# A linear-attention, FFN and soft-MoE kernel: the scheduler keeps TensorE's form, and the last block's weights use five, then six buffers

## The chip, the core and the metric

One NeuronCore of a Trainium2 chip runs the whole kernel. It has five engines that work in parallel, each through its own instruction queue in order: TensorE (PE, matmuls), VectorE (DVE), ScalarE (ACT), GpSimd (POOL) and SyncE (SP, which here only issues DMAs; ACT issues some too). The 16 DMA engines carry all queues' transfers. The metric is the device time of the kernel in microseconds (us); less is better.

## What is computed

The input goes through three stages. First, linear attention with positive features for 4 x 8 heads of 576 tokens, 64 wide, 128 features:

```python
h = proj - sq                       # proj = x @ omega.T, sq = |x|^2 / 2, x scaled by 64 ** -0.25
phi = np.exp(h - np.max(h, axis=-1, keepdims=True)) / np.sqrt(m)
kv = np.einsum('bhsm,bhsd->bhmd', k_p, v)
...
num / den                           # q_p @ kv over q_p @ sum(k_p), plus 1e-06
```

The result, 2304 tokens of 512 values, goes through a gated FFN with 1536 hidden values, and that through a soft mixture of 8 experts with 4 slots each:

```python
gate = 1.0 / (1.0 + np.exp(-(x @ w_gate)))
x = gate * (x @ w_val) @ w_out
logits = x @ phi
d = softmax(logits, axis=0)         # over tokens: what goes into each slot
slot_input = d.T @ x
slot_out[e] = np.maximum(slot_input[e] @ w1[e], 0.0) @ w2[e]
c = softmax(logits, axis=1)         # over slots
out = c @ slot_out
```

## The kernel before

**Tiling.** The FFN runs over five blocks of tokens: four of 512 (blocks 0 to 3) and a last one, block 4, of 256. Each block has 12 steps `f`, one for 128 of the hidden values. In a step, `gate` (PSUM tile `ga`), `val` (`va`) and `down` (`o0` to `o3`) each make 12 products: four chunks times the three of `three`, which multiplies numbers split into a high and a low part of type fp32r (hi by hi, hi by lo, lo by hi). So a step is three groups of twelve products, 512 columns wide, 256 in block 4; a step's `down` is done after the next step's `gate` and `val`. The soft-MoE's work on a finished block (`chunk_logits`, `chunk_x2`, `chunk_ltT`, `chunk_slot`) is done while the next block's FFN runs, in plain fp32, as are attention's products and all transposes. In the trace a plain fp32 product leaves two records, an fp32r product or a transpose one.

**Weights.** The weights of a step are three parts: gate (part 0), value (1), down (2). For the last blocks they come from the DRAM scratch `wscr` into `WR` (name `ws`), six slots of 256 KB. `split_w` makes the high part on ACT (or DVE) and the low one on POOL (or DVE) into tiles `w`, which the products read. In block 4 (`i >= LAST`) the parts come one by one in the order of the list `USE`: f0's gate and value, f1's, f0's down, f2's gate and value, f1's down, f3's gate (number 8) and value (9), f2's down, and so on. Only four slots serve them: number m goes into slot `m % 4`, and `split_w` of a part issues the load of the part four numbers later:

```python
def load_part(m):
    if m < len(USE):
        W[USE[m]] = WR[:, m % 4, :]
        SP.dma_start(out=W[USE[m]], in_=wscr[USE[m][0] % NF][:, USE[m][1], :])
```

The other two slots (4 and 5) are given by `free_early` to the experts' second weights W2, twelve microseconds of planned time into block 4, along with one buffer `gt`.

**The block's transposition.** `chunk_x2` transposes block 3's result with four DVE instructions, writes each quarter to DRAM (`xscr`) and reads it back (`x2T<-xscr`). Both go on SP's queue, between the weight loads; `chunk_slot`'s four products, 512 columns wide, need what is read back.

**What sets the order.** Every instruction is recorded by `Plan` and put in order by `schedule()` before the kernel is built. It is a list scheduler that simulates the five engines with the prices of `cost()`. Each instruction has a key (its stream's planned time less a lead), and `pick` takes the ready one of the lowest key on the engine that is free. `cost()` charges TURN = 0.2 extra for a bundle (`together`) of PE work with fewer than 128 rows, and 0.12 for products with 64 output partitions; no price hangs on what was issued before. A DMA is planned to land at 340 GB/s plus 2.0 us. All instructions are issued by one line of `issue`, so every row of the trace reads L413 (L449 in the changed kernel), and tile names tell the steps apart. W1, the experts' first weights, is loaded by `load_w1` on ACT's queue in pieces of 512 KB (`XT<-in_w` among them), W2 by `load_w2` on SP's. `join_slots` joins the blocks' running softmax before the tail.

## Time and profile before

| | |
|---|---|
| median of 3 runs (677.37, 679.89, 680.16) | 679.89 us |
| the profiled execution, its own time | 678.63 us |
| its span, first to last instruction | 676.8 us |
| PE busy | 658.8 us, 97% |
| DVE, ACT, POOL busy | 442.5, 429.0, 279.9 us |
| DMA moved | 147.90 MB, mean 219 GB/s |
| mean granted TensorE clock | 0.995 of full speed |

The share of busy time is an average over stages: attention and FFN run together in the first 200 us, then the FFN with the soft-MoE's chunks; block 4 lies at about 557 to 624 us; behind it is the experts' tail. The timeline lists groups of instructions of one kind with their start, their length from first start to last end, a count of records, and in brackets the idle time of the engine before the group with what ended it. Groups on PE overlap by some tenths at their ends, since matmuls are pipelined and their ends are modelled; the distance from one start to the next is what a group costs.

### The profile page before, as it was taken

How to read it: one execution, taken by the hardware profiler on the slowest of the kernel's cores; microseconds unless marked ns; L12 is line 12 of the kernel's file. 1: busy time of each engine (PE TensorE's matmuls, PEld its weight loads, DVE VectorE, ACT ScalarE, POOL GpSimd, SP SyncE). 2: the span in 40 equal slices, each digit the busy share in tenths (PEclk: the TensorE clock that was granted, in tenths of full speed). 3: DMA queues.
4: the chain of work that ended last, by engine and by line, in shares of the span. 5: the costliest groups of instructions: out<-in, count | busy, mean ns of one | idle time of the engine just before them, and what ended most of it. 6: DMA issues, size and time to landing. Idle time of an engine off the chain costs nothing.

```text
span 676.8 us, 12606 instructions
## 1 busy us (share of the span) xinstructions
PE 658.8 (97%) x4340; PEld 529.8 (78%) x4340; DVE 442.5 (65%) x1309; ACT 429.0 (63%) x965; POOL 279.9 (41%) x244
## 2 busy tenths in 40 slices
PE   7999999999999999999999999999999999999995
PEld 6676777878888888887888888788888788798663
DVE  3899999899997476666576555567343336575323
ACT  5899898888886765667566766455444445575012
POOL 1465445465444443444345343444444444443100
PEclk9999999999999999999999999999999999899998
DMA  8889876787975345834395222789833339966978
GB/s 285 314 269 341 277 252 226 250 273 242 309 252 171 123 153 193 243 126 162 101 260 167 89 67 75 255 295 334 251 93 101 101 107 310 284 207 233 406 303 240
DMA packets 57103, 147.90 MB, mean 219 GB/s; under 512 B 6096, under 2 KB 14032, under 8 KB 57040
## 3 DMA queue, kind: packets, MB, share of 16 engines
q1 hardware_dynamic: 51232, 129.74, 58.2%
q10 hardware_dynamic: 5808, 17.37, 7.7%
q8 instruction: 34, 0.56, 0.3%
q14 instruction: 29, 0.24, 0.1%
HBM read 128.73 MB, written 18.35 MB: 217 GB/s over the span
## 4 chain that ended last, share of the span: by engine, by line
PE 88%; DMA 4%; DVE 3%; ACT 2%; issue 1%; SPq 1%; POOL 0%; DVEq 0%; ACTq 0%; POOLq 0%
PE o L413 26%; PE ga L413 23%; PE va L413 23%; PE fl L413 16%; DMA g<-in_tok 1%; ACT g L413 1%; DMA ws<-wscr 1%; DVE g L413 1%; DMA g<-in_wall 1%; DMA xscr<-x 1%; DVE x2T L413 1%; SPq L413 1%; POOL g L413 0%; DVE g1b L413 0%; DVE ga_a L413 0%
## 5 line engine op out<-in xcount | busy, mean ns | idle before, releaser
L413 POOL TENSOR_TENSOR w<-ws,w 128x512 fp32r<-128x512 f32 x133 | 174.7, 1315 | 243.4 <-ACT w L413 115.6
L413 PE MATMUL ga<-XT,w 128*128 128x512 f32 (+1 forms) x720 | 169.8, 378 | 1.8 <-ACT w L413 0.8
L413 PE MATMUL va<-XT,w 128*128 128x512 f32 (+1 forms) x720 | 168.6, 376 | 1.8 <-ACT w L413 1.8
L413 PE MATMUL o<-gt,w 128*128 128x512 f32 (+1 forms) x720 | 167.4, 376 | 0.8 <-DVE gt L413 0.8
L413 PEld LDWEIGHTS o<-gt,w 128*128 128x128 f32 x720 | 124.3, 189 | 28.8 <-issue 3.7
L413 PEld LDWEIGHTS ga<-XT,w 128*128 128x128 f32 x720 | 124.4, 190 | 27.2 <-issue 1.9
L413 PEld LDWEIGHTS va<-XT,w 128*128 128x128 f32 x720 | 125.0, 190 | 26.5 <-issue 2.4
L413 ACT ACTIVATE w<-ws 128x512 fp32r<-128x512 f32 x113 | 71.0, 628 | 62.3 <-PE o L413 22.5
L413 PE MATMUL fl<-g,g 64*128 64x128 f32 (+4 forms) x686 | 83.9, 314 | 2.2 <-DVE g L413 0.8
L413 ACT ACTIVATE ga_a<-ga_a 128x512 f32<-128x512 f32 (+1 forms) x120 | 69.9, 583 | 19.3 <-DVE ga_a L413 18.1
L413 PEld LDWEIGHTS fl<-g,g 64*128 64x128 f32 (+2 forms) x686 | 61.5, 183 | 22.7 <-issue 6.1
L413 ACT ACTIVATE g<-g 128x128 f32<-128x128 f32 (+3 forms) x203 | 72.3, 408 | 10.9 <-DVE g L413 6.3
L413 ACT ACTIVATE ga_a<-ga 128x512 f32<-128x512 f32 (+1 forms) x60 | 33.3, 554 | 68.0 <-PE ga L413 67.9
L413 DVE SCALAR_TENSOR_TENSOR ga_a<-ga,ga_a 128x512 f32<-128x512 f32 (+1 forms) x60 | 38.0, 634 | 42.0 <-ACT ga_a L413 41.9
L413 DVE CAST w<-ws 128x512 fp32r<-128x512 f32 x49 | 20.9, 426 | 54.9 <-PE ga L413 37.5
L413 DVE TENSOR_TENSOR ga_a<-va,ga_a 128x512 f32<-128x512 f32 (+1 forms) x60 | 38.0, 633 | 20.5 <-ACT ga_a L413 17.6
L413 ACT ACTIVATE x2T<-g 128x512 f32<-128x512 f32 x72 | 45.4, 665 | 4.0 <-DVE x L413 4.0
L413 ACT ACTIVATE g1b<-g1b,g 128x128 f32<-128x128 f32 x128 | 40.5, 389 | 5.0 <-DVE g L413 4.9
L413 ACT ACTIVATE ga_a<-ga_a,one_b 128x512 f32<-128x512 f32 (+1 forms) x60 | 40.7, 678 | 1.3
L413 DVE TENSOR_SCALAR x2T<-x2T 128x512 f32<-128x512 f32 (+1 forms) x72 | 38.6, 549 | 2.8 <-ACT x2T L413 2.7
L413 DVE TENSOR_TENSOR g<-fl,g 64x288 f32<-64x288 f32 (+3 forms) x61 | 29.3, 482 | 15.0 <-ACT g L413 13.9
L413 POOL TENSOR_TENSOR g<-g 128x640 f32<-128x640 f32 (+1 forms) x22 | 25.9, 1176 | 31.1 <-DVE g L413 17.5
(197 smaller groups left out, 789.5 us busy)
## 6 DMA issues: line engine op xcount, KB each, us to landing
ws<-wscr SPq DMA_DIRECT2D x42, 512.0 KB, 3.7
ws<-wscr SPq DMA_DIRECT2D x78, 256.0 KB, 3.1
g<-in_wall SPq DMA_DIRECT2D x36, 512.0 KB, 4.9
g<-in_von SPq DMA_DIRECT2D x16, 640.0 KB, 5.8
wscr<-x SPq DMA_DIRECT2D x36, 256.0 KB, 4.8
g<-in_qkT SPq DMA_DIRECT2D x15, 576.0 KB, 5.1
g<-in_tok SPq DMA_DIRECT2D x15, 576.0 KB, 5.3
g<-in_w ACTq DMA_DIRECT2D x16, 512.0 KB, 6.2
```

The source lines that it names most:

```text
L413: ins = getattr(self.eng[e], method)(*a, **k)
```

## The change

The change has two halves.

In the scheduler, `form()` gives each PE instruction its form: operand rows, output partitions, and whether it is fp32r. The new `pick_pe` takes the lowest key as before; but if that one's form differs from the form of the last instruction put on PE, it takes, among the ready ones of the last form, the lowest whose key is no more than STAY = 2.0 later, if there is one. In the simulated time a change of rows or output partitions costs SWITCH = 0.18 and a change to fp32r ROUND = 0.09; TURN and the 0.12 are gone from `cost()`'s PE prices. The planned landing of a write to `xscr` gets BACK = 1.5 more.

In the weights of block 4, the parts are taken from a list `todo` in the order of `USE`, and each goes into whichever slot has come free. Five loads are issued where four were (slots 0 to 4), a sixth (slot 5) after the split of the step before. Slots 4 and 5 stay in use until a part with number 15 (`WIDE`) or later has been split out of them; then `free_early` gives both to W2. `free_early` no longer hands out the `gt` buffer.

```diff
 LATE8 = 0.3
 FLOOR = 8
-EARLY = 12.0
+WIDE = 15
 SQP = [0, 0, 1, 1, 1, 0, 1, 0]
...
 SIZE = {F32: 4, F32R: 4, I32: 4, U32: 4, I64: 8}
 HOP = 0.16
+SWITCH = 0.18
+STAY = 2.0
+ROUND = 0.09
+BACK = 1.5
 TURN = 0.2
 ROWS = 4
...
         if method == "together":
-            return TURN * (eng == "PE" and kw["parts"][0][2][0].ap[0][1] < 128) + sum(self.cost(eng, a[1], a[3], o, i)[0] for a, o, i in kw["parts"]), False
+            return sum(self.cost(eng, a[1], a[3], o, i)[0] for a, o, i in kw["parts"]), False
         o = outs[0] if outs else None
         n = self.free(o) if o is not None else 0
...
                 return max(0.43 * n / 256, 0.055) / 4, False
             if o.ap[0][1] == 64:
-                return max(n / 600.0, 0.21) / 2 + 0.12, False
+                return max(n / 600.0, 0.21) / 2, False
             return max(0.222, n / 600.0) * (ins[0].ap[0][1] / 128 if o.ap[0][1] == 128 else 1.0), False
         ni = max([n] + [self.free(a) for a in ins])
...
         return 0.06, False
+    def form(self, i):
+        alts, _, _, _, outs, ins, _ = self.ops[i]
+        if alts[0][0] != "PE":
+            return None
+        kw = alts[0][3]
+        if "parts" in kw:
+            _, outs, ins = kw["parts"][0]
+        return ins[0].ap[0][1], outs[0].ap[0][1], ins[0].dtype == F32R
     def schedule(self):
...
             return self.cost(e, alt[1], alt[3], outs, ins)
+        forms = [self.form(i) for i in range(n)]
+        form = [(128, 128, False)]
+        def pick_pe():
+            while ready["PE"] and taken[ready["PE"][0][1]]:
+                heapq.heappop(ready["PE"])
+            if not ready["PE"]:
+                return None
+            x = ready["PE"][0]
+            if forms[x[1]] != form[0]:
+                same = [y for y in ready["PE"] if y[0] <= x[0] + STAY and forms[y[1]] == form[0] and not taken[y[1]]]
+                x = min(same, default=x)
+            ready["PE"].remove(x)
+            heapq.heapify(ready["PE"])
+            return x[1]
         def pick(e):
+            if e == "PE":
+                return pick_pe()
             shared = e in ("DVE", "POOL") and port > now + 1e-9
...
                     alt = next(a for a in alts if a[0] == e)
                     c, held = self.cost(e, alt[1], alt[3], outs, ins)
+                    if e == "PE" and forms[i] != form[0]:
+                        c += SWITCH * (forms[i][:2] != form[0][:2]) + ROUND * (forms[i][2] > form[0][2])
+                        form[0] = forms[i]
                     if held:
                         port = now + c
...
                         nb *= SIZE[outs[0].dtype]
                         dma = max(dma, now) + nb / 340e3
-                        end = max(dma, now + nb / 340e3) + 2.0
+                        end = max(dma, now + nb / 340e3) + 2.0 + BACK * outs[0].tensor.name.startswith("xscr")
                     order.append((now, i, alt))
                     free_at[e] = now + c
...
     WR = T([128, 6, 512], "ws")
     W, Q, WS, G = {}, {}, {}, {}
+    spent = []
     cw = {}
...
     USE = [(i + (p < 2), p) for i in range(LAST - 1, NB * NF) for p in range(3) if LAST <= i + (p < 2) < NB * NF]
-    def load_part(m):
-        if m < len(USE):
-            W[USE[m]] = WR[:, m % 4, :]
+    slot, todo = {}, list(range(len(USE)))
+    def load_part(k):
+        if todo:
+            m = todo.pop(0)
+            slot[USE[m]] = k
+            W[USE[m]] = WR[:, k, :]
             SP.dma_start(out=W[USE[m]], in_=wscr[USE[m][0] % NF][:, USE[m][1], :])
...
                 W[i, p] = a[:, p, :]
         elif i == LAST:
-            for m in range(4):
-                load_part(m)
+            for k in range(5):
+                load_part(k)
     def load_q(n):
...
         lo_of(t[:, 1, :], w, t[:, 0, :], ("DVE",) if end else SITE["lw"])
         WS[i, part] = t
+        if (i, part) == (LAST - 1, 2):
+            load_part(5)
         if i >= LAST:
-            load_part(USE.index((i, part)) + 4)
+            k = slot[i, part]
+            if k < 4 or USE.index((i, part)) < WIDE:
+                load_part(k)
+            else:
+                spent.append(k)
+                if len(spent) == 2:
+                    free_early()
     def up_passes(i, part, tag):
...
     def free_early():
+        lead, plan.lead = plan.lead, LEAD["ex"]
         free.append(WR[:, 4:6, :].rearrange("p a c -> p (a c)"))
-        free.extend(pieces("gt", 2, 1))
         load_w2()
+        plan.lead = lead
     def free_halves():
...
             jobs += [(start + 10.0 + 12 * k, "ex", load_w1) for k in range(6)]
         if j == NB - 1:
-            jobs += [(start + 10.0, "ex", load_w1), (start + 40.0, "ex", free_more), (start + EARLY, "end", free_early),
+            jobs += [(start + 10.0, "ex", load_w1), (start + 40.0, "ex", free_more),
                      (start + span * 0.9, "end", free_halves), (start + span * 0.85, "m2", join_slots)]
         start += span
     jobs += moe_jobs(NB * NF, start, 1.0)
```

What moves, as the order of instructions on three engines tells it. SP, block 4, around the writes of block 3's transposed result (`xscr`) and the reads of it (`x2T<-xscr`), before; `ws<-wscr` are weight parts, `gt`, `x` and `more` W2 pieces:

```order
L413 DMA gt<-in_w 128x1024
L413 DMA xscr_75<-x_726 128x512
L413 DMA xscr_76<-x_726 128x512
L413 DMA xscr_77<-x_726 128x512
L413 DMA xscr_78<-x_726 128x512
L413 DMA ws<-wscr 128x512
L413 DMA x2T<-xscr_75 32x4x512
L413 DMA ws<-wscr 128x512
L413 DMA x2T<-xscr_76 32x4x512
```

The same place in the changed kernel:

```order
L449 DMA ws<-wscr 128x512 x8
L449 DMA gt<-in_w 128x1024
L449 DMA xscr_75<-x_726 128x512
L449 DMA xscr_76<-x_726 128x512
L449 DMA xscr_77<-x_726 128x512
L449 DMA xscr_78<-x_726 128x512
L449 DMA ws<-wscr 128x512 x2
L449 DMA x2T<-xscr_75 32x4x512
L449 DMA ws<-wscr 128x512
L449 DMA x2T<-xscr_76 32x4x512
```

Counted over block 4, eight weight parts stood ahead of the first write and now ten, nine ahead of the first read and now twelve.

PE, block 4, steps f3 to f5 (`w_733` is f4's gate part), with `chunk_slot`'s products `fl<-x2T,dt`, before:

```order
L413 MATMUL ga<-XT_105,w_733 128x256 x2
L413 MATMUL fl<-ident,cs 128x128
L413 MATMUL ga<-XT_105,w_733 128x256 x10
L413 MATMUL fl<-x2T,dt 32x512 x3
L413 MATMUL va<-XT_105,w_736 128x256 x2
L413 MATMUL fl<-x2T,dt 32x512
L413 MATMUL o_718<-gt,w_741 128x256 x2
```

The place of the same products in the changed kernel, six steps later (`w_768` is f9's gate part):

```order
L449 MATMUL ga<-XT_105,w_768 128x256 x12
L449 MATMUL va<-XT_105,w_771 128x256 x12
L449 MATMUL fl<-x2T,dt 32x512 x4
L449 MATMUL o_718<-gt,w_772 128x256 x3
L449 MATMUL o_719<-gt,w_772 128x256 x3
```

The four products stand in a row and later. In the same way block 3's sixteen logits' products, fifteen and one before, stand in a row, and the PE work of `join_slots` has moved from the middle of block 4 to its last step. Over the whole program PE changes rows or output partitions 127 times instead of 136 (five of the nine within the first 78 us, four in block 4), and type alone 121 times instead of 154.

ACT, the start of block 4 (`w_704` is f1's gate part, `x2T<-o` takes block 3's result out of PSUM), before:

```order
L413 DMA XT<-in_w 128x1024
L413 ACTIVATE ga_a<-ga 128x256
L413 ACTIVATE w_704<-ws 128x512
L413 ACTIVATE ga_a<-ga_a 128x256
L413 ACTIVATE ga_a<-ga_a,one_b 128x256
L413 ACTIVATE x2T<-o_614 128x512
```

The same place in the changed kernel:

```order
L449 DMA XT<-in_w 128x1024
L449 ACTIVATE ga_a<-ga 128x256
L449 ACTIVATE w_704<-ws 128x512
L449 ACTIVATE ga_a<-ga_a 128x256
L449 DMA XT<-in_w 128x1024
L449 ACTIVATE ga_a<-ga_a,one_b 128x256
```

A third piece of W1 is issued there that came behind the cast of `w_733` before; a fourth has moved to the cast of `w_722` (f1's down part). About twelve low parts of weights, most of them in block 4, go from POOL to DVE.

## Rows read from the trace of the kernel before

**Rows 1.** The page's first part: engine, busy us, share of the span, instructions

```profile
PE 658.8 (97%) x4340; PEld 529.8 (78%) x4340; DVE 442.5 (65%) x1309; ACT 429.0 (63%) x965; POOL 279.9 (41%) x244
```

**Rows 2.** Windows: stretch in us, busy us by engine, PEclk, DMA share, GB/s

```profile
27.00:64.00 37.00, 34.61 (x227) 25.52 (x225) 35.09 (x150) 34.10 (x98) 21.68 (x24) 1.00 0.88 295
...
150.00:200.00 50.00, 50.00 (x244) 41.19 (x244) 47.86 (x93) 42.40 (x83) 22.77 (x17) 1.00 0.82 276
...
570.00:582.00 12.00, 9.48 (x65) 9.01 (x64) 7.39 (x25) 6.55 (x17) 4.01 (x4) 0.86 1.03 271
```

**Rows 3.** Timeline of PE: start, length, operation, count, [idle before <-releaser], all in us

```profile
571.88 1.60 PE L413 MATMUL o<-gt,w 128*128 128x256 f32 x12
573.32 0.27 PE L413 MATMUL fl<-ident,lt 128*128 128x128 f32 x1
574.35 0.51 PE L413 MATMUL ga<-XT,w 128*128 128x256 f32 x2 [0.76 <-ACT w L413]
...
576.84 0.39 PE L413 MATMUL va<-XT,w 128*128 128x256 f32 x1 [1.76 <-ACT w L413]
577.06 2.11 PE L413 MATMUL ga<-XT,w 128*128 128x256 f32 x10
578.97 2.26 PE L413 MATMUL va<-XT,w 128*128 128x256 f32 x11
581.07 1.60 PE L413 MATMUL o<-gt,w 128*128 128x256 f32 x12
```

**Rows 4.** Timeline of ACT, last block, the cast of f3's gate weights

```profile
573.67 0.63 ACT L413 ACTIVATE w<-ws 128x512 fp32r<-128x512 f32 x1 [0.88 <-DMA ws<-wscr]
```

**Rows 5.** Timeline of SP's queue, issues of weight loads, last block

```profile
560.59 2.03 SPq L413 DMA_DIRECT2D ws<-wscr  x2
...
567.88 0.32 SPq L413 DMA_DIRECT2D ws<-wscr  x1
```

**Rows 6.** Windows of five microseconds, last block

```profile
565.00:570.00 5.00, 5.00 (x61) 4.27 (x61) 3.16 (x8) 2.84 (x6) 3.44 (x3) 1.00 0.98 363
```

**Rows 7.** Timeline of PE, last block, the logits' products

```profile
566.84 1.07 PE L413 MATMUL fl<-x2T,phs 128*32 128x128 f32 x30
567.91 0.73 PE L413 MATMUL o<-gt,w 128*128 128x256 f32 x4
568.57 0.41 PE L413 MATMUL fl<-x2T,phs 128*32 128x128 f32 x2
568.91 0.50 PE L413 MATMUL ga<-XT,w 128*128 128x256 f32 x2
```

**Rows 8.** Timeline of PE, last block, the products of chunk_slot

```profile
584.13 1.06 PE L413 MATMUL fl<-x2T,dt 128*32 128x512 f32 x6
585.12 0.50 PE L413 MATMUL va<-XT,w 128*128 128x256 f32 x2
585.55 1.05 PE L413 MATMUL fl<-x2T,dt 128*32 128x512 f32 x2
586.53 0.86 PE L413 MATMUL o<-gt,w 128*128 128x256 f32 x5
```

**Rows 9.** Timeline of PE, the block before the last, around its chunk_slot

```profile
523.43 2.88 PE L413 MATMUL ga<-XT,w 128*128 128x512 f32 x12
526.15 2.88 PE L413 MATMUL va<-XT,w 128*128 128x512 f32 x12
528.96 1.07 PE L413 MATMUL fl<-x2T,dt 128*32 128x512 f32 x8
529.96 3.02 PE L413 MATMUL o<-gt,w 128*128 128x512 f32 x12
```

**Rows 10.** Timeline of PE, a gate-value step with attention's transposes on both sides

```profile
255.32 3.02 PE L413 MATMUL va<-XT,w 128*128 128x512 f32 x12
```

**Rows 11.** PE's waits: what waits for what, us in total, times, longest us

```profile
PE o L413 <- DVE gt L413: 0.8, 1, 0.8
```

**Rows 12.** DMA at 559 to 564 us: queue, packets, MB, share of 16 engines

```profile
q10 hardware_dynamic: 138, 0.51, 28.1%
```

## The prediction

> **What bounds the kernel now.** I began with the page's busy shares: TensorE (PE) is busy 658.8 of 676.8 us, 97%, so little can be gained by ending waits, and most of what can be gained must come out of time that counts as busy [rows 1]. The windows of busy time per engine show where the 97% is something else than work [rows 2]. From 27 to 64 us VectorE (DVE) and PE are both near full, at 150 to 200 us PE is full and DVE has 47.86 of 50; and at 570 to 582 us, in the first part of the last token block, PE is busy for 9.48 of 12 us, and its granted clock is 0.86 in the mean, so part of it at the lower of its two levels (1.2 and 2.4 GHz).
>
> PE's timeline there gives the prices [rows 3]. Twelve fp32r products of 128x256 take 1.44 us from start to start (571.88 to 573.32), so one is 0.120. PE then waits 0.76 us and 1.76 us for a cast of weights on ScalarE (ACT), and after the second wait it runs slowly: ten products take 1.91 us (577.06 to 578.97) and eleven take 2.10 (to 581.07), where 1.20 and 1.32 would be due. ACT's row shows why the cast is late: it waits for the weights' load out of DRAM [rows 4]. That load (f3, part 0) was issued on SP's queue only at 567.88, behind four writes that wait for DVE's transposes, and the cast began 5.8 us later [rows 4, 5]. Meanwhile the 16 DMA engines are 98% busy at 363 GB/s [rows 6].
>
> **A: two more weight buffers ahead of the writes.** Before, eight parts of block 4's weights are issued ahead of the first write to DRAM, now ten; f3's gate and value parts, for which PE waited, are the two that were added. In the trace a pair goes out at 560.59 to 562.6 [rows 5]; the next pair on the two added slots can follow at once, and with landings of up to 8 us (above the 5.8 of the row) it is there at 568.6 to 570.6, against 573.3, when PE comes for it. So I take both waits as gone, and with them the slow clock that follows the idle time. The stretch from 571.88 to 581.07 is 9.19 us long. In it lie 36 products (36 x 0.120 = 4.32) and three transposes (about 0.3 as an estimate, at a tenth each beside the printed 0.27 for one, which overlaps): 4.6 due, 4.6 too much. I take 4.4, since changes between transposes and products stay in it: **-4.4**, upper end of the gain -4.6.
>
> **B: groups that are no longer cut.** In the last block the logits go in as 15 products and, behind four others, one more [rows 7]. Fifteen take 1.07 us, 0.07 each; the lone one takes 0.34 and the four `o` between them 0.66 where 0.48 is due. Unsplit, 0.27 + 0.18 = 0.45 goes. `chunk_slot` goes in as three products, two `va`, one product [rows 8]: 0.99 + 0.43 + 0.98 = 2.40 us, where four in a row take 1.00 us in the block before (528.96 to 529.96) [rows 9] and two `va` 0.24: 1.16 goes. Together **-1.6**. The order has 16 and 4 in a row now, so this does not hang on A.
>
> **C: fewer changes of shape elsewhere.** Over the whole order, changes of the operands' rows or output partitions go from 136 to 127. Four of these nine lie in the last block and are in B, five lie before about 78 us. The price: twelve products of 128x512 take 2.72 us from start to start (523.43 to 526.15), 2.81 when another shape follows (to 528.96), and those behind one print 3.02 where 2.88 is usual, so 0.09 + 0.14 = 0.23 for there and back, 0.12 a change, and more by what lies in the group itself [rows 9]. At up to 0.2 each, five give 0 to -1.0. In that stretch DVE and PE share the limit [rows 2], so I take half, **-0.5**.
>
> **D: fewer changes of type alone.** Changes between fp32r products and fp32 transposes of one shape go from 154 to 121, some 16 pairs. Twelve products between two groups of transposes print 3.02 us [rows 10], where undisturbed ones print 2.88 [rows 9]: 0.14 a pair at most, and a part of it is the transposes' own end, which stays. Nothing to 0.14 for 16 pairs is 0 to -2.2. I take 0.03 a pair, near the lower end, because the row leaves nothing else to pay once that end is counted off: **-0.4**.
>
> The Trainium skill, "TensorEngine Tiling (Array Packing)", section "Key Properties", says that changing the tiling mode drains TensorE and names no change of type; by it D would be nothing and the sum 0.4 us higher. No row here separates the two.
>
> **E: the next load that is late.** Even with six slots, f5's gate part waits for a slot and stands on SP's queue behind the reads of the transposed block. In the trace these follow the load of 567.88 [rows 5]; as an estimate it goes out about 573. Landing 5.8 to 8 us later it arrives at 579 to 581. With A's waits gone, PE has run f3 (three groups from 573.3, 4.3 us) and f4's three, another 4.3, and asks for it near 582. The margin is about a microsecond; ends 0 and +2.0 (the larger wait of [rows 3] and a little slow clock): I take **+0.4**.
>
> **F: the join.** `join_slots` has its six small PE operations moved from the middle of the last block to its last step. There PE waits 0.8 us today for DVE's `gt` [rows 11]. Filling that wait is worth up to -0.8; but one of the moved products waits for a copy that DVE makes after `gt`, and three small DVE operations come before it, so it can also cost up to +1.0 (the wait once more and the copy). I take **0**.
>
> **G: the rest of the order.** Before 200 us the scheduler's new costs reshuffle attention, FFN and DVE work. No row prices it; I take 0, with ends of +/-1.5. Twelve lo-splits go from POOL to DVE, mostly in the last block, where DVE has 7.39 busy of 12 us [rows 2]: hidden. W2 pieces on the SP queue start sooner or later by some us but are used 50 us on: nothing.
>
> **Sum.** -4.4 - 1.6 - 0.5 - 0.4 + 0.4 = -6.5 on the profiled execution's 678.63 us: 672.1. That execution lies 1.26 us under the median of 679.89, so the median should be **673.4**.
>
> **Rivals.** *The load is late anyway.* ACT's queue now issues two more 512 KB W1 loads beside the casts of the block's first weights, where before they came behind f4's; with the two weight parts 1.5 MB more go into a stretch in which the DMA engines are already 98% busy [rows 6]. At 363 GB/s 1.5 MB are 4.1 us: landings of 5.8 become 10, f3's gate arrives at 570 to 573, and the parts behind it (f3's down part and f4's, issued after the writes as before) slip by as much. Then most of A stays: 673.4 + 4.4 = 677.8 us, no measurable change. Against it: the parts are ahead of the writes, and the transposed block is not needed until far later now. Chance 0.24.
> The Trainium skill, "DMA: Bandwidth & Descriptors", section "Queues, rings and completion order", says that a DMA engine takes the queues it has work for in turn, packet by packet; by it ACT's loads take their turns beside SP's and slow them, as this rival has it. The trace agrees as far as it goes: at 559 to 564 us ACT's queue took 28.1% of the engines' time beside SP's [rows 12].
>
> *The early part gets slower.* A product is now passed over for one of the same form that is due up to 2 us later by the plan. Before 100 us the passed-over ones are attention steps on which DVE, and through it the next PE work, waits; PE idles 2.39 us at 27 to 64 [rows 2]. Each pass that makes PE idle counts in full. Some 5 shape changes and 16 pairs of type changes were removed, 21 passes if each is one; slower than before by the bound below needs 673.4 + 9.9, so 0.47 us of new idle time for each pass. At 0.6 each it would be 673.4 + 12.6 = 686.0 us. Against it: most of the removed changes are of type alone, and at 150 to 200 us PE is full although DVE is at 96% [rows 2]. Chance 0.10.
>
> **Chances and range.** The forecast has 0.66. A measurement of this kernel tells about 0.5% from no change, 3.4 us, so faster begins under 676.5 and slower over 683.3. The forecast's cases fall in faster, the first rival in same, the second in slower: 0.66, 0.24, 0.10. For the low end I take the better ends of A, C and F, D at 1.0 and G in part: -4.6 - 1.6 - 1.0 - 1.0 - 0.8 - 1.5 = -10.5, 669.4 on the median's scale, put at 669.5. For the high end the first rival with E or F at a little over 1 us more: 679.0. The 0.10 of the second rival and a little below the low end stay out.
>
> **What would show it.** In the trace of the changed kernel: A right, if PE's waits for ACT's `w` of 1.8 and 0.8 us are gone, the granted clock at 570 to 582 is 1.00 and ACT's casts of weights there name no DMA; B, if the 16 logits and the 4 slot products each stand in one row of about 1.1 and 1.0 us; C and D, if the twelve-product rows of 3.02 become fewer, and block 3's products that began at 523.43 begin 0.5 to 1.5 us earlier; E and F, if new waits of `ga` for `w` (f5) or of `o` for `gt` and `lt` stay under 1 us. The forecast is wrong if ACT still waits for `ws` there, or if PE's busy time before 100 us falls while the last block begins later.

## The result

The changed kernel takes **682.54 us** (median of 11 runs, 680.92 to 687.00), the kernel before 679.08 us on the same chips (11 runs, 677.37 to 680.32). The ratio is 1.0052 with a 95% interval of 1.0035 to 1.0068: half a per cent slower. Forecast were 673.4 us, with 669.5 to 679.0 as the range. The profiled execution of the changed kernel took 684.56 us with a span of 682.8 us, so it stands 2 us above its own median; that has to be kept in mind when its rows are read. The changed kernel's runs spread over 6 us and those of before over 3; the three longest, 684.56 to 687.00 us, have a mean granted clock of 0.986 to 0.989, the five shortest, all under 682 us, 0.995 to 0.997.

The page of the changed kernel, its busy times and the granted clock in 40 slices of 17 us:

```profile
PE 659.2 (97%) x4340; PEld 530.2 (78%) x4340; DVE 444.1 (65%) x1322; ACT 430.8 (63%) x964; POOL 265.5 (39%) x232
...
PEclk9997999999999999999999999999999999999998
```

PE is busy for 659.2 us, as before [rows 1]; all that was lost is idle time, and work at the lower clock, which counts as busy. The 7 in the clock's row stands at 51 to 68 us, where the row of before had a 9.

Where the time went shows best from three marks in PE's timeline: the first FFN product, the first product of block 4, and the first logits product of the tail. In the kernel before:

```profile
27.19 0.48 PE L413 MATMUL ga<-XT,w 128*128 128x512 f32 x1
...
557.30 1.60 PE L413 MATMUL ga<-XT,w 128*128 128x256 f32 x12
...
623.63 1.07 PE L413 MATMUL ga<-x2T,phs 128*32 128x128 f32 x16
```

And in the changed kernel:

```profile
29.76 0.50 PE L449 MATMUL ga<-XT,w 128*128 128x512 f32 x1 [0.70 <-ACT w L449]
...
566.46 1.59 PE L449 MATMUL ga<-XT,w 128*128 128x256 f32 x12
...
630.12 1.07 PE L449 MATMUL ga<-x2T,phs 128*32 128x128 f32 x16
```

Block 4 begins 9.16 us later (566.46 against 557.30). It takes 63.66 us instead of 66.33: 2.67 us were gained in it. The tail takes 52.7 us instead of 53.2. With the first FFN product at 29.76 us instead of 27.19, the 9.16 are 2.57 us of start-up and 6.59 us between the first FFN product and block 4. The start-up's share can't be put down to the change: three kernels of the study below whose instructions stand in the order of before up to there and far beyond began their first FFN product at 28.23, 28.93 and 29.53 us. So the middle distance is the measure: 530.11 us before, 536.70 after.

**The early part.** The windows of the changed kernel that answer to [rows 2] (stretch, length, busy us of PE, PEld, DVE, ACT and POOL, granted clock, DMA share, GB/s):

```profile
27.00:64.00 37.00, 33.73 (x205) 25.14 (x204) 31.02 (x135) 33.26 (x95) 18.58 (x21) 0.95 0.90 303
64.00:100.00 36.00, 34.87 (x216) 26.32 (x215) 31.73 (x113) 30.12 (x76) 14.49 (x13) 0.91 0.70 234
...
570.00:582.00 12.00, 11.79 (x109) 10.66 (x108) 9.52 (x22) 6.88 (x17) 5.11 (x4) 1.00 0.95 332
```

The second of them in the kernel before:

```profile
64.00:100.00 36.00, 35.97 (x224) 25.54 (x225) 34.45 (x115) 32.77 (x80) 15.98 (x15) 1.00 0.79 266
```

At 27 to 64 us PE is busy for 33.73 us where it was 34.61, at a clock of 0.95 in the mean instead of 1.00; at 64 to 100 us for 34.87 where it was 35.97, at 0.91 instead of 1.00. PE's timeline at that place (with its waits in brackets), and finer windows:

```profile
57.93 1.16 PE L449 MATMUL fl<-g,g 64*128 64x128 f32 x14 [0.88 <-DVE g L449]
...
61.23 1.22 PE L449 MATMUL ga<-XT,w 128*128 128x512 f32 x2 [1.49 <-POOL XT L449]
...
64.09 2.08 PE L449 MATMUL fl<-g,g 64*128 64x128 f32 x16
67.23 4.15 PE L449 MATMUL fl<-g,g 128*128 128x128 f32 x20 [1.06 <-ACT g L449]
...
73.84 1.16 PE L449 MATMUL fl<-g,g 64*128 64x128 f32 x16
```

```profile
60.00:62.00 2.00, 0.77 (x2) 0.67 (x3) 2.00 (x18) 1.59 (x5) 0.94 (x2) 0.63 0.96 354
62.00:64.00 2.00, 2.00 (x6) 1.16 (x4) 1.05 (x8) 2.00 (x7) 1.25 (x1) 0.50 0.70 254
...
72.00:74.00 2.00, 2.00 (x11) 1.40 (x11) 1.30 (x4) 1.63 (x3) 0.56 (x1) 1.00 0.81 206
```

PE waits 0.88 us for DVE in attention's chain and 1.49 us for POOL, which splits attention's result for the FFN; from about 61 us the granted clock is 0.50, the lower level of 1.2 GHz. In it sixteen records of 64 rows by 128 columns take 2.08 us, where sixteen take 1.16 at full clock (73.84); the twenty of 128x128 take 4.15. The next wait, 1.06 us, falls into the same time, and full clock is back before 72 us. Between the first FFN product and block 4 PE's waits add up to 4.9 us, and to 2.3 before. In the ten microseconds at 0.50 PE was busy for about 8.5; half of that, 4.3 us, is an estimate of what the lower clock cost. These two make up the 6.59.

**Block 4.** The changed kernel's timeline there:

```profile
576.00 1.08 PE L449 MATMUL fl<-x2T,phs 128*32 128x128 f32 x32
...
582.94 1.69 PE L449 MATMUL ga<-XT,w 128*128 128x256 f32 x12
...
592.39 1.46 PE L449 MATMUL o<-gt,w 128*128 128x256 f32 x10 [0.90 <-POOL w L449]
595.22 1.70 PE L449 MATMUL ga<-XT,w 128*128 128x256 f32 x12 [1.37 <-DVE ga_a L449]
...
615.66 1.06 PE L449 MATMUL fl<-x2T,dt 128*32 128x512 f32 x8
```

The sixteen logits and the four `chunk_slot` products stand in one row each, 1.01 and 1.00 us to the next start. The waits of [rows 3] are gone at f3 (582.94), and the granted clock is 1.00 all through block 4. But PE now waits 0.90 us in f3's `down` (592.39) and 1.37 us at f5's gate (595.22). ACT's and SP's rows tell why:

```profile
590.30 0.63 ACT L449 ACTIVATE w<-ws 128x512 fp32r<-128x512 f32 x1 [2.58 <-DMA ws<-wscr]
...
593.48 0.63 ACT L449 ACTIVATE w<-ws 128x512 fp32r<-128x512 f32 x1 [1.82 <-DMA ws<-wscr]
```

```profile
583.16 0.35 SPq L449 DMA_DIRECT2D x<-in_w  x1
584.12 16.18 SPq L449 DMA_DIRECT2D ws<-wscr  x10
```

The casts of f3's down part and of f5's gate part wait 2.58 and 1.82 us for their loads. The load of f5's gate is the first of the ten behind a W2 piece of 512 KB, and behind the reads of the transposed block: issued at about 584, there when the cast begins at 593.48, some nine microseconds later.

### The profile page after: what moved, and what is told of

It is laid out like the page before. It is cut to its first block, busy times and chain, and to the rows that moved or that the text cites. A ratio compares the mean times of both kernels' runs of the same rounds, so it can differ in the third digit from the quotient of the medians.

```text
span 682.8 us, 12583 instructions
## 1 busy us (share of the span) xinstructions
PE 659.2 (97%) x4340; PEld 530.2 (78%) x4340; DVE 444.1 (65%) x1322; ACT 430.8 (63%) x964; POOL 265.5 (39%) x232
## 5 line engine op out<-in xcount | busy, mean ns | idle before, releaser
L449 POOL TENSOR_TENSOR w<-ws,w 128x512 fp32r<-128x512 f32 x122 | 158.9, 1303 | 239.2 <-ACT w L449 108.1
L449 PE MATMUL ga<-XT,w 128*128 128x512 f32 (+1 forms) x720 | 167.8, 377 | 3.7 <-POOL XT L449 1.5
L449 PE MATMUL va<-XT,w 128*128 128x512 f32 (+1 forms) x720 | 166.7, 375 | 0.8 <-POOL w L449 0.4
L449 PE MATMUL o<-gt,w 128*128 128x512 f32 (+1 forms) x720 | 165.3, 374 | 2.0 <-POOL w L449 1.7
L449 ACT ACTIVATE w<-ws 128x512 fp32r<-128x512 f32 x109 | 68.4, 628 | 66.2 <-PE o L449 22.0
L449 PE MATMUL fl<-g,g 64*128 64x128 f32 (+4 forms) x686 | 86.8, 320 | 3.8 <-ACT g L449 1.8
L449 ACT ACTIVATE g<-g 128x128 f32<-128x128 f32 (+4 forms) x203 | 71.6, 409 | 11.9 <-DVE g L449 7.2
L449 DVE CAST w<-ws 128x512 fp32r<-128x512 f32 x53 | 22.5, 425 | 54.6 <-PE ga L449 38.3
L449 POOL TENSOR_TENSOR XT<-g,XT 128x64 fp32r<-128x64 f32 (+2 forms) x45 | 30.3, 684 | 36.5 <-DVE XT L449 6.8
L449 DVE TENSOR_TENSOR w<-ws,w 128x512 fp32r<-128x512 f32 x40 | 31.9, 798 | 16.3 <-ACT w L449 15.5
```

Of the source, the lines that this page charges most:

```text
L449: ins = getattr(self.eng[e], method)(*a, **k)
```

## The experiments

**Theory S**: the scheduler's half lost the time, in the early part, and the weights' half gained. **Theory W**: the weights' half costs as well. And within S: **P**, passing a due product over for one of the last form makes attention's chain wait (the prediction's second rival), against **K**, the plan's new prices do it. "To block 4" is the distance from the first FFN product to block 4's first product, "block 4" from there to the tail's logits, both in us and from one execution of each kernel, the profiled one; its own time stands beside them ("profiled"), to be held against the median. The ratio is to the kernel before, run beside it.

| run | what it is | median, us | ratio, 95% interval | profiled, us | to block 4 | block 4 |
|---|---|---|---|---|---|---|
| before | | 679.08 | 1 | 678.63 | 530.11 | 66.33 |
| after | | 682.54 | 1.0052 (1.0035, 1.0068) | 684.56 | 536.70 | 63.66 |
| weights_only | weights' half alone | 680.15 | 1.0012 (0.9996, 1.0028) | 683.38 | 530.26 | 68.29 |
| scheduler_only | scheduler's half alone | 685.06 | 1.0091 (1.0069, 1.0113) | 682.76 | 533.49 | 67.09 |
| prices_only | after, no preference | 683.01 | 1.0055 (1.0033, 1.0076) | 684.05 | 535.43 | 65.00 |
| preference_only | after, old prices | 678.66 | 0.9991 (0.9976, 1.0006) | 678.59 | 529.20 | 67.59 |
| old_until_180 | after, old scheduler early | 676.02 | 0.9943 (0.9926, 0.9959) | 675.63 | 528.72 | 65.46 |
| switch_added | after, old prices kept too | 683.37 | 1.0058 (1.0036, 1.0079) | 685.02 | 536.00 | 65.34 |
| turn_removed | after, SWITCH = ROUND = 0 | 680.89 | 1.0016 (0.9997, 1.0034) | 679.68 | 532.37 | 65.06 |
| loads_moved | preference_only, five loads later | **674.11** | 0.9915 (0.9888, 0.9943) | 672.40 | 530.05 | 61.07 |
| weights_moved | weights_only, five loads later | 675.33 | 0.9948 (0.9930, 0.9965) | 675.22 | 530.67 | 61.04 |
| before_loads_moved | before, seven loads later | 681.80 | 1.0029 (1.0014, 1.0044) | 682.26 | 530.12 | 67.93 |
| early_old_moved | old_until_180, five loads later | 674.97 | 0.9937 (0.9917, 0.9956) | 676.72 | 529.57 | 63.63 |
| price_016 | after, SWITCH = 0.16 | 680.13 | 1.0009 (0.9993, 1.0024) | 680.07 | 531.07 | 64.82 |
| price_020 | after, SWITCH = 0.20 | 679.30 | 1.0008 (0.9991, 1.0025) | 683.05 | 533.06 | 65.93 |
| round_0 | after, ROUND = 0 | 679.15 | 1.0003 (0.9989, 1.0018) | 679.23 | 531.13 | 65.53 |

### The two halves apart

weights_only is the changed kernel with the scheduler of before (BACK, the planned landing of the writes, stays):

```diff
-SWITCH = 0.18
-STAY = 2.0
-ROUND = 0.09
+SWITCH = 0.0
+STAY = -1.0
+ROUND = 0.0
...
+            return TURN * (eng == "PE" and kw["parts"][0][2][0].ap[0][1] < 128) + sum(...), False
...
+                return max(n / 600.0, 0.21) / 2 + 0.12, False
```

> The changed kernel with the old scheduler (no preference for the last form, no SWITCH or ROUND, TURN and 0.12 back), so only the last block's weights in five, then six buffers and BACK are left. The instructions of PE are in the order of before up to the last block. Theory S (the scheduler's half lost the time, before 200 us): A is gained without B, so 3 to 4.5 us under before, 674.5 to 676.5 us, and the last block begins at 557.3 us as before. Theory W (the weights' half costs time as well, by its crowding of the DMA engines): 679 us or more, with ACT still waiting for ws in the last block.

It takes 680.15 us, no different from before, and its early part is that of before: S is right that this half does not lose the time there, but the gain A that S expected is missing. Time and waits are those that W expected; that this half costs is not shown, since the interval holds 1. Block 4 is even longer, 68.29 us, though in an execution that is the longest of the twelve, 3.2 us above their median. Its timeline:

```profile
576.19 1.69 PE L449 MATMUL ga<-XT,w 128*128 128x256 f32 x12
579.07 1.69 PE L449 MATMUL va<-XT,w 128*128 128x256 f32 x12 [1.18 <-DVE ga_a L449]
...
589.59 2.93 PE L449 MATMUL ga<-XT,w 128*128 128x256 f32 x12 [3.08 <-DVE ga_a L449]
```

DVE and SP in the same run:

```profile
588.78 0.43 DVE L449 CAST w<-ws 128x512 fp32r<-128x512 f32 x1 [2.82 <-DMA ws<-wscr]
```

```profile
578.27 0.35 SPq L449 DMA_DIRECT2D x<-in_w  x1
579.53 6.78 SPq L449 DMA_DIRECT2D ws<-wscr  x6
```

f3's gate comes without a wait, its value part waits 1.18 us, and at f5 PE stands for 3.08 us; the row behind that wait is 2.93 us long where f3's is 1.69, at a granted clock of 0.50 (590 to 595 us). The wait is put down to DVE's `ga_a`: that is the operation that frees the bank of f4's gate, and it is queued on DVE behind the cast of f5's value part, which waited 2.82 us for its load. **The wait was moved, not removed**: from f3's weights to f5's. It is no oddity of one long execution: preference_only below, profiled at its median, has it in the same place:

```profile
585.75 2.93 PE L449 MATMUL ga<-XT,w 128*128 128x256 f32 x12 [3.68 <-DVE ga_a L449]
```

The windows of weights_only say what the load waited for:

```profile
565.00:570.00 5.00, 5.00 (x59) 4.79 (x61) 4.52 (x11) 3.25 (x7) 0.63 (x1) 1.00 0.99 371
...
580.00:585.00 5.00, 5.00 (x44) 5.00 (x43) 3.34 (x9) 2.35 (x5) 2.58 (x2) 1.00 1.05 251
```

The DMA engines are as full as before [rows 6], at 371 GB/s, and behind it come the four reads of the transposed block (256 KB each), during which the engines are full at only 251 GB/s. Ten to twelve parts, three or four W1 and W2 pieces and the reads have to go through here, and the order in which they go decides who waits.

scheduler_only is the kernel before with `form`, `pick_pe` and the new prices, and nothing of the weights; against the changed kernel:

```diff
+EARLY = 12.0
-BACK = 1.5
+BACK = 0.0
...
-            for k in range(5):
-                load_part(k)
+            for m in range(4):
+                load_part(m)
...
-            jobs += [(start + 10.0, "ex", load_w1), (start + 40.0, "ex", free_more), 
...
+            jobs += [(start + 10.0, "ex", load_w1), (start + 40.0, "ex", free_more), (start + EARLY, "end", free_early),
```

> The kernel before with the scheduler's half alone (form, pick_pe, SWITCH, ROUND; TURN and 0.12 gone; BACK 0), weights in four buffers as before. Theory S: slower than the changed kernel by what the weights' half gives, 685 to 688 us, the last block beginning 7 to 10 us later than in the kernel before. Theory W: 679 us or less, since the half that costs is undone.

685.06 us, slower than the changed kernel: the early loss is the scheduler's. (S had put the start of block 4 at 7 to 10 us later than before; in the profiled execution, which lies 2.3 us under the median, it is 3.8.) Its PE order is the changed kernel's up to block 4, and yet its distance to block 4 is 533.49 us and not 536.70. The 3.2 us between two executions of one order all arise within PE's first 500 records, where the clock stood at 0.50 for some 3 us in this one and for ten in the other. So 6.59 us is what the order cost in one of its longer executions, not a fixed price.

### Preference or prices

prices_only sets STAY to -1, so that nothing is passed over; preference_only keeps STAY and sets the prices to those of before:

```diff
-STAY = 2.0
+STAY = -1.0
```

> The changed kernel with STAY = -1, so that no product is ever passed over for one of the last form; the prices of the plan (SWITCH, ROUND, TURN and 0.12 gone) stay. Theory P (passing over costs, since attention's chain waits): the early loss is gone, 674 to 677 us, first gate products of step 1 at 64 to 65 us. Theory K (the new prices cost, since they change the planned times on which all queues are ordered): 681 to 687 us, step 1 at 68 us or later.

```diff
-SWITCH = 0.18
+SWITCH = 0.0
-ROUND = 0.09
+ROUND = 0.0
...
+            return TURN * (eng == "PE" and kw["parts"][0][2][0].ap[0][1] < 128) + sum(...), False
...
+                return max(n / 600.0, 0.21) / 2 + 0.12, False
```

> The changed kernel with SWITCH = ROUND = 0 and TURN and 0.12 back, so that the plan's prices are those of before and only the preference for the last form (STAY = 2.0) is left of the scheduler's half. Theory P: 681 to 687 us, step 1's first gate products at 68 us or later. Theory K: 674 to 677 us, step 1 at 64 to 66 us.

683.01 and 678.66 us. The preference costs nothing in the early part (529.20 us, and 530.05 in loads_moved, against 530.11), the prices do (535.43). **K stands and P falls**, though the second time lies outside both ranges: K's counted on a gain in block 4 that isn't there (67.59 us). And the preference alone lays as new an order as the change does: of PE's first 1100 records some 330 stand elsewhere than in the kernel before, some 290 in the changed kernel. So a new order does not lose time by being new. Which of the prices it is, two more runs ask. switch_added has the old prices beside the new ones:

```diff
-                return max(n / 600.0, 0.21) / 2, False
+                return max(n / 600.0, 0.21) / 2 + 0.12, False
...
+            return TURN * (eng == "PE" and kw["parts"][0][2][0].ap[0][1] < 128) + sum(...), False
```

> The changed kernel with TURN and 0.12 back, and SWITCH, ROUND and the preference on top. If the new prices of a change are what slows the early part: 681 to 686 us. If taking TURN and 0.12 away does it (attention's half-row products planned too short): 676 to 680 us, like the run with the preference alone (678.66).

turn_removed has neither:

```diff
-SWITCH = 0.18
+SWITCH = 0.0
-ROUND = 0.09
+ROUND = 0.0
```

> The changed kernel with SWITCH = ROUND = 0, TURN and 0.12 gone: attention's products are planned shorter and a change costs nothing. If the removal slows the early part: 681 to 686 us. If the new prices do: 676 to 680 us. If both this one and the one with the prices added are slow, any change of the plan's prices reshuffles the early part for the worse, and the old order was the lucky one.

Both are slow early, by 5.9 and 2.3 us, and in switch_added the granted clock is 1.00 from 27 us to block 4, so the loss does not need the lower clock. So is it the direction (changes planned dearer, half-row products planned cheaper), or is any order worse there that is laid by other prices than the old ones? Three runs with one number changed:

```diff
-SWITCH = 0.18
+SWITCH = 0.16
```

> The changed kernel with SWITCH = 0.16 for 0.18 and nothing else. If the prices slow the early part by their direction (changes planned dearer), a ninth less of one price moves the time little: 681.5 to 683.5 us. If it is a matter of chance how a new order falls there, it can land anywhere between 678 and 686 us, off the changed kernel by 1.5 us or more.

```diff
-SWITCH = 0.18
+SWITCH = 0.20
```

> The changed kernel with SWITCH = 0.20 for 0.18. With 0.16 it ran in 680.13 us, with 0.18 in 682.54. If the loss grows with the price: 683.5 to 686 us. If it is chance: off that line, 679 to 682 us or above 686.

```diff
-ROUND = 0.09
+ROUND = 0.0
```

> The changed kernel with ROUND = 0, so that a change of type is planned at what the row of added products showed for it (nothing). If the wrong price of a type change is what spoils the early order: 677 to 680 us. If any change of the prices lays a new order there, and a good one is chance: anywhere from 678 to 685 us, with step 1 to 35 late by a few microseconds again.

With SWITCH at 0.16, 0.18 and 0.20 the kernel takes 680.13, 682.54 and 679.30 us: no line through them. Without the price for a type change, which is wrong (below), it takes 679.15. Each of the eight kernels with new prices is behind in the early part, by 1.0 to 6.6 us, and how far does not follow the size of a price. (The four kernels with the old early order took 530.11 to 530.67 us, and two executions of one other order, in preference_only and loads_moved, differ by 0.85, so the two least losses, 1.0 us, are hardly more than scatter.) In the changed kernel the new prices lay a new order from about PE's 40th instruction on, through all five engines, and none of the orders that new prices laid was as quick there as the old one. In all, turn_removed, price_016, price_020 and round_0 are not shown to be slower than the kernel before: their intervals hold 1. That is as far as the runs go: what makes these orders slower than that of before and that of preference_only was not shown, nor which price is to blame.

old_until_180 keeps the old scheduler for the first 180 us of planned time:

```diff
-            if forms[x[1]] != form[0]:
+            if forms[x[1]] != form[0] and now >= AFTER:
...
-                        c += SWITCH * (forms[i][:2] != form[0][:2]) + ROUND * (forms[i][2] > form[0][2])
+                        c += (now >= AFTER) * SWITCH * (forms[i][:2] != form[0][:2]) + (now >= AFTER) * ROUND * (forms[i][2] > form[0][2])
```

> The changed kernel with the old prices and no preference until 180 us of planned time, so PE's first 822 instructions are in the order of before, and the new scheduler from there. Theory K (the prices hurt only the stage in which attention and FFN run together): that loss is gone, 676 to 679 us. Rival (the prices reshuffle whatever they touch, or the loss sits in the last block): 681 us or more.

676.02 us, 6.5 us less than the changed kernel (one of its twelve runs took 1656 us and is left out of the ratio; the cause is not known): the loss is in the stage where attention and FFN run together, and the new scheduler does no harm behind it.

### The crowded loads

loads_moved is preference_only with two W1 pieces and three W2 pieces held back until f5's gate part is loaded in the plan:

```diff
+LATER = 566.0
...
+                plan.floor = LATER if e == E - 1 and c > 1 else 0.0
                 ACT.dma_start(out=W1[e][c], in_=w1[e, :, 1024 * c:1024 * c + 1024])
...
-        plan.floor = plan.t
+        plan.floor = LATER
         load_w2()
```

> The run with the preference alone (678.66 us) with three pieces of W2 and two of W1, 512 KB each, held back until after the load of f5's gate part in the plan (566 us of planned time). Theory C (crowding: the wait for f3's weights was not removed but moved to f5's, since the DMA engines are full from 560 to 590 us): PE's wait of 3.7 us at f5 and the slow clock behind it are gone, 672 to 675 us. Rival (f5's load is late for its slot and its place on SP's queue, not for the other transfers): wait stays above 2.5 us, 677 to 680 us. A third way: the pieces land too late for the experts' tail, which gives back 1 to 3 us there.

674.11 us, 0.85% under before: the fastest kernel of the study. Its timeline at the start of block 4 and at the gates of f2, f3 and f5, and SP's queue:

```profile
556.78 1.60 PE L450 MATMUL ga<-XT,w 128*128 128x256 f32 x12
...
567.96 0.40 PE L450 MATMUL ga<-XT,w 128*128 128x256 f32 x2
...
572.87 1.70 PE L450 MATMUL ga<-XT,w 128*128 128x256 f32 x12
...
582.36 1.60 PE L450 MATMUL ga<-XT,w 128*128 128x256 f32 x12
```

```profile
571.35 11.30 SPq L450 DMA_DIRECT2D ws<-wscr  x8
582.70 0.43 SPq L450 DMA_DIRECT2D x<-in_w  x1
```

The gates of f3 and f5 start without a wait, and so does f4's. The parts go out in one run of eight behind the reads, and the W2 piece `x` follows them at 582.70, where in the changed kernel it stood ahead. Block 4 takes 61.07 us, 5.26 less than before, and the tail (52.75 us) does not miss the pieces. The preference is not what gives most of it. The same without it:

```diff
-STAY = 2.0
+STAY = -1.0
```

> The run with the weights' half alone (680.15) with the five pieces of W1 and W2 held back (566 us of planned time); no preference, no new prices. If the five and six buffers and the emptier DMA engines together are what helps, and the preference for a form gives little: 673 to 675.5 us. If the preference gives most of the 674.11 of the run that had both: 677 us or more.

weights_moved has no preference and no new prices, and block 4 takes 61.04 us in it; 675.33 us in all (the intervals of the two overlap). And emptier engines alone don't help either. In the kernel before, the lines of loads_moved and, besides, the pieces that it frees early:

```diff
     def free_early():
...
+        plan.floor = LATER
         load_w2()
+        plan.floor = 0.0
```

> The kernel before, four buffers and old scheduler, with seven pieces of W1 and W2 held back until f5's gate part is loaded in the plan. If crowding of the DMA engines alone makes f3's weights late: their load lands in about 4 us instead of 5.8, the waits of 0.8 and 1.8 us and the slow clock go, 674 to 676 us. If the place behind the four writes makes it late and the two added buffers are what helps: waits stay above 1.5 us, 677 to 680 us.

Its PE timeline, and a window:

```profile
575.10 1.70 PE L414 MATMUL ga<-XT,w 128*128 128x256 f32 x12
578.99 0.51 PE L414 MATMUL va<-XT,w 128*128 128x256 f32 x2 [2.19 <-DVE ga_a L414]
```

```profile
575.00:580.00 5.00, 2.52 (x19) 2.08 (x18) 2.16 (x7) 1.22 (x3) 1.17 (x1) 1.00 1.04 258
```

With four buffers and seven pieces held back, PE comes to f3's gate without a wait but stands for 2.19 us at f3's value part. Its load is issued after the reads have begun, and those fill the engines (share 1.04) at 258 GB/s. 681.80 us, a little slower than before and outside both ranges; a later part's cast then waits 2.22 us for its load and PE 1.49 us behind it (at 607 and 608 us), where the pieces held back are loaded. So **two conditions have to be met together**: the parts issued ahead of the writes, which takes the added buffers (alone: 680.15 us), and no other bulk ahead of f5's parts (alone: 681.80; both: 675.33). The change met the first. Which of the five pieces, those on SP's queue or those on ACT's, was in the way was not tried.

early_old_moved puts the two findings together, old_until_180 with the loads held back to its own plan's time for f5:

```diff
+LATER = 574.0
```

> The run with the old scheduler until 180 us of planned time (676.02) and the five pieces of W1 and W2 held back as in the run with the loads moved (674.11), until 574 us of planned time. If the two gains lie in different places they add: the last block saves another 2 to 4 us, 672 to 674 us. If the wait for f5 was small there already: 675 to 677 us.

674.97 us, less than hoped, and by the two intervals no different from old_until_180: block 4 takes 63.63 us there, and a cast of f3's down part still waits 2.32 us for its load. That the gains add was not shown.

### The price of a change of form

Products without use were added behind the end of the kernel before, in blocks and mixed two to one, and run once:

```diff
+        for kind in ("type", "out", "rows"):
+            r(24)
+            for _ in range(12):
+                one(kind)
+            r(12)
+            for _ in range(12):
+                r(2)
+                one(kind)
```

> The kernel before with a row of products added behind its end: 24 fp32r products, 12 others and 12 fp32r in a block, then 24 fp32r and 12 others mixed two to one, for others that are transposes (type alone changes), products with 32 output partitions, and products with 64 rows. By the sum of the prediction a mix costs over the same products in a block: type alone 12 pairs x 0.03 = 0.4 us (bounds 0 to 1.7), output partitions 12 x 0.23 to 0.4 = 2.8 to 4.8 us, rows the same. If type costs as much as shape, 2.8 us or more for the first.

PE's timeline: a block of twelve and the start behind it, then one round of the mix, for transposes, for 32 output partitions (two records each) and for 64 rows:

```profile
690.32 1.47 PE L413 MATMUL ga<-ident 128*128 128x128 f32 x12
691.54 1.91 PE L413 MATMUL ga<-w 128*128 128x256 f32 x14
...
694.33 0.27 PE L413 MATMUL ga<-ident 128*128 128x128 f32 x1
...
694.68 0.27 PE L413 MATMUL ga<-ident 128*128 128x128 f32 x1
...
700.17 2.81 PE L413 MATMUL ga<-ident,phs 128*32 128x128 f32 x24
702.91 1.94 PE L413 MATMUL ga<-w 128*128 128x256 f32 x14
...
705.55 0.41 PE L413 MATMUL ga<-ident,phs 128*32 128x128 f32 x2
...
706.32 0.41 PE L413 MATMUL ga<-ident,phs 128*32 128x128 f32 x2
...
716.62 2.94 PE L413 MATMUL ga<-ident 64*128 64x128 f32 x24
719.49 1.94 PE L413 MATMUL ga<-w 128*128 128x256 f32 x14
...
722.62 0.50 PE L413 MATMUL ga<-w 128*128 128x256 f32 x2
...
723.47 0.50 PE L413 MATMUL ga<-w 128*128 128x256 f32 x2
```

A transpose in a block takes 1.22 / 12 = 0.102 us; a round of one transpose and two fp32r products takes 0.35, and 0.102 + 2 x 0.120 = 0.342: **a change of type costs nothing** that these rows can show (0.01 us for there and back). With 32 output partitions: 2.74 / 12 = 0.228 in a block, a round 0.77, so 0.30 us for there and back. With 64 rows: 0.239 and 0.85, so 0.37 us. SWITCH, 0.18 for one change, was thus about right (half of there and back is 0.15 and 0.185), and ROUND wrong; round_0, whose prices are the nearest to these rows, is no faster than the kernel before for it.

## Why the prediction was wrong

Two steps failed. **G** put the new early order at nothing; it cost up to 6.59 us. And **E** put what comes in the place of A's waits at 0.4 us; it was 2.3 us in the changed kernel and more in two others. The prediction's last sign of being wrong came true: PE is busy for 89.43 us of the first 100 instead of 93.74, and block 4 begins later.

- **What bounds the kernel**: right. PE's busy time did not move, and all that moved were waits and the clock behind them.
- **A**: right at f3, where the waits and the slow clock went as foretold. What came in their place (**E**) is the step that failed for block 4. It was taken at 0.4 us with 2.0 as its end, on landings of 5.8 to 8 us; f3's down part and f5's gate part took 8.3 and 9.3, waits of 0.90 and 1.37 us came back in the changed kernel, and of 3.08 us with a slow clock in weights_only. The margin of "about a microsecond" was worked out from a landing time of before, while the change itself put more into the same full stretch. The first rival had this mechanism, and its price, most of A, fits weights_only, where no gain is left (680.15 us). It looked for the delay at f3's gate and what is issued next, however, and the larger part came at f5. That the changed kernel's total falls into this rival's class, no clear change, is no credit to it: there a part of A's gain stayed, and the early part lost more than that.
- **The queue rule** beside that rival was not what made f5's parts late. In the changed kernel ACT's W1 loads did take 39.2% of the engines' time at 564 to 576 us, beside SP's 45.5%, but the parts issued then landed in 5.3 to 6.1 us, in time. At 572 to 597 us SP's own queue held almost all and ACT's 7.5% (queue, packets, MB, share):

```profile
q1 hardware_dynamic: 3378, 6.67, 91.4%
```

  What stood ahead of f5's parts was SP's own order, with a W2 piece and the reads. The Trainium skill, "DMA: Bandwidth & Descriptors", section "Queues, rings and completion order", has an engine take in turn the queues that it has work for; the first of these two stretches agrees with that, and in the second there was little to take turns with.
- **B**: right. The slot products take 1.00 us in a row, as put down. For the logits 0.45 us was put down: in loads_moved, where the sixteen and then the four `o` go in ahead of f2, f2's gate starts 11.18 us after block 4's first product (556.78 to 567.96), 0.43 less than the 11.61 of before. In the sum of block 4, -4.4 - 1.6 + 0.4 = -5.6 was forecast; the changed kernel gained 2.67 us, and loads_moved, with the new wait gone, 5.26.
- **C**: the price was right (0.23 and more for there and back against 0.30 and 0.37 measured), but the five changes in the early part were paid for by waits there.
- **D**: wrong. 16 pairs at 0.03 us were counted as a gain; the measured price is 0.01 us there and back, so by these rows the 0.14 us by which [rows 10] is longer is no price of the change. The Trainium skill, "TensorEngine Tiling (Array Packing)", section "Key Properties", names a drain for a change of the tiling mode and none for a change of type; the rows agree on the type (0.01 us). Whether the changes of rows and output partitions that cost 0.30 and 0.37 us are changes of that mode, no run here shows.
- **F**: right within its ends, and small: the tail's first logits came at 630.12 with no wait over 0.3 us in the join.
- **G** is the step that turned the sign. "No row prices it; I take 0, with ends of +/-1.5" covers an order that was laid anew from about PE's 40th instruction on, in a stage where DVE, ACT and PE are all over 90% busy (27 to 64 us, [rows 2]). It cost 1.0 to 6.6 us on the way to block 4 in the eight kernels with new prices, in the changed kernel as waits and as time at the lower clock. Why these orders are slower stays open.
- **The second rival** named the place and the sign (its loss, 9.9 us or more, was larger than any measured), but its mechanism was wrong: passing products over cost nothing. The prices, which the prediction treated as a means only, moved the order. Its 0.10 stood on too narrow a cause; the case "the early order gets worse, for whatever reason" should have had more.

## What to carry to other kernels

A list scheduler's price is not a local thing: a number that prices one step better lays a new order over the whole program. Where several engines are nearly full a new order can be worse, as it was with new prices eight times here, or as good, as it was with the preference alone, and the better price does not tell which. So limit a new rule to the stage it is meant for, and cost "the rest of the order" with wide ends. When a late load is cured by issuing it sooner, the bytes are not gone: look which load lands last in the same full stretch after the cure, and move what is not yet needed out of it. A wait for one engine can be a wait for a load that another operation on that engine's queue stands for.

## What the runs showed of the hardware that was not expected

- A change between fp32r products and fp32 transposes, both with 128 rows and 128 output partitions, cost 0.01 us there and back; a change to 32 output partitions or to 64 rows 0.30 and 0.37 us (price_of_a_change).
- After waits of 0.88 and 1.49 us the granted clock stood at 0.50 for about ten microseconds, though PE was busy in most of them (the changed kernel).
- With four reads of 256 KB into 32 partitions under way, the DMA engines were full (share 1.05 and 1.04) at 251 and 258 GB/s (weights_only, before_loads_moved); with loads into 128 partitions, at 371 (weights_only, 565 to 570 us).
- The start, up to the first FFN product, took 27.19, 28.23, 28.93 and 29.53 us in four executions with the same instructions there; in the last of them (weights_only) the granted clock was 0.66 in the mean at 15 to 20 us, in the first three 1.00.
